# The block of r, k and w that a chunk loads: 128 rows of three padded pieces in place of 112 unbroken rows

## The chip, the cores and the metric

The kernel runs on one core of a Trainium2 chip. The metric is the device time of one execution in microseconds, so lower is better. Five engines work side by side: TensorE (PE, whose weight loads are listed apart as PEld), VectorE (DVE), ScalarE (ACT), GpSimd (POOL) and SyncE (SP, which here issues nearly all DMAs). Sixteen DMA engines move the data between DRAM and the on-chip memory SBUF, which has 128 rows (partitions).

## What is computed

Two stages follow each other. The first is a recurrence over 768 positions for 4 batches and 8 heads of width 48, with a state of 48 by 48 for each batch and head that is multiplied by w at each position. The second is a feed-forward layer on the 3072 by 384 result, with a hard-swish between its two products.

```python
for t in range(S):
    kt, vt, rt, wt = (k[:, :, t], v[:, :, t], r[:, :, t], w[:, :, t])
    cur = np.einsum('bhd,bhe->bhde', u[None] * kt, vt)
    y[:, :, t] = np.einsum('bhd,bhde->bhe', rt, state + cur)
    state = wt[:, :, :, None] * state + np.einsum('bhd,bhe->bhde', kt, vt)
...
h = x @ w_in                                 # (3072, 384) @ (384, 2048)
g = h * np.clip(h + 3.0, 0.0, 6.0) / 6.0
out = g @ w_out                              # (3072, 2048) @ (2048, 384)
```

## The kernel before

**Chunks.** The 768 positions of a batch are cut into 6 chunks of 128, so there are 24 chunks. Chunks of two batches alternate, and four chunks make one block of 512 tokens for the feed-forward layer. For a chunk, r, k and w are needed with the 48 channels of a head on partitions. Four heads lie on partitions 0 to 47 and the other four on 64 to 111, so 112 partitions (`PR`) are used, and `P` is 4. The host writes this layout into one DRAM array, `feat`: a chunk has 112 rows, and each row holds 512 values of r, 512 of k, and 520 of w (eight halves of 64 positions, each with a leading 0) and a last zero, 1545 floats or 6180 bytes without a break.

**The load of a chunk** is `load_feat`, line 343. It is one DMA on SP (line 349) of 112 rows of 6180 bytes into a buffer named `feat_in`. Chunk 0 is split: its w first (line 346, 521 floats of a row), then its r and k (line 354, 1024 floats of a row). Three buffers of the name `feat_in` take turns; later in the program the same buffers also take 128-row, 6144-byte reloads of w and of the weights for a range check (lines 919 and 924), which DVE reduces. Beside the block, a chunk loads its v (`v_in`, line 361, 128 rows) and, from chunk 9 on, r and k with positions on partitions (`rk_in`, line 366).

**What reads the block.** DVE runs two scans over w, `E` from the back (line 428) and `W` from the front (line 437). `K` is k times E (line 448) and `R` is r times W (line 452); both are on DVE for chunks 0 to 6 and on POOL from then on. For chunks 0 to 8 DVE also makes `rk`, r times k (line 461), from the block; PE reduces it with u (line 473, into `ps`). PE then makes the scores of a chunk (line 498), turns K (line 514), and makes the chunk's output (lines 576 and 585, into `y_ps` or a `bank`) and its addition to the state (line 598).

**Weights.** `w_in` and `w_out` arrive as 64-bit floats in pieces named `bits` (line 391, 768 KB each), and are rebuilt as 32-bit floats on ACT (lines 400 and 405, into `more`) and DVE (line 411 into `top`, line 415 into `w_in` or `w_out`). These DMAs stand on SP's queue between the loads of the first chunks.

**The feed-forward layer.** Block 0 multiplies by w_in and w_out directly (lines 714 and 733). Later blocks use sums of blocks of the operands and fewer products (lines 829 and 884), with the sums and the hard-swish on DVE and ACT (lines 776 to 869).

**What sets the order.** Every step is added to a plan with its engine, an assumed duration and its needs. The order of all steps is one fixed table of numbers, `ORDER`, so each engine's order of instructions doesn't depend on the plan's durations. In the first 60 us of the plan, PE gets matmuls of the identity matrix without use (line 1260, into `bankS`) wherever the plan expects it to wait; their number is set when the program is built.

**A second path.** A flag that the range check sets chooses `general_path`, a slower way for extreme values of w. With these inputs it is not run.

Of the kernel before, what the change touches and what calls it, by code (L numbers as in the profile page):

```python
# [8 lines left out]
F32 = mybir.dt.float32  # L9
# [11 lines left out]
L = 128  # L21
HL = L // 2
GP = 64
# [220 lines left out]
def fast_path(tc, feat, tok, wflat, ub, ug, moe_w_in, moe_w_out, out, flag, n_chunks):  # L244
# [3 lines left out]


    nc = tc.nc  # L250
    NT, PR, nf = feat.shape
    HD = tok.shape[3]
    D = PR - GP
    H = HD // D
    P = H // 2
# [11 lines left out]
    with ExitStack() as ctx:  # L267
        const = ctx.enter_context(tc.tile_pool(name="const", bufs=1))
        io = ctx.enter_context(tc.tile_pool(name="io", bufs=3))
# [6 lines left out]
        chunk_of = [(i // NSEQ * 2 + i % 2) * n_chunks + i % NSEQ // 2 for i in range(NT)]  # L276
# [8 lines left out]
        st = [dict() for _ in range(NT)]  # L285
# [50 lines left out]


        n = P * L
        plan.ring("feat", 3)
        plan.ring("tok", 3)  # L340
        plan.ring("rk_in", 2)

        def load_feat(i):
            a = io.tile([PR, nf], F32, name="feat_in")
            if i == 0:
                nc.sync.dma_start(out=a[:, 2 * n:], in_=feat[chunk_of[i], :, 2 * n:])
                nc.scalar.dma_start(out=u_col, in_=ug)
            else:
                nc.sync.dma_start(out=a, in_=feat[chunk_of[i]])
            st[i].update(a=a, r=a[:, :n].rearrange("q (x t) -> q x t", t=HL),  # L350
                         k=a[:, n:2 * n].rearrange("q (x t) -> q x t", t=HL), w=a[:, 2 * n:])

        def load_rest():
            nc.sync.dma_start(out=st[0]["a"][:, :2 * n], in_=feat[chunk_of[0], :, :2 * n])

        def load_u():
            nc.sync.dma_start(out=u_bc, in_=ub.to_broadcast([128, HD]))
# [612 lines left out]
        def when(i):  # L970

            bk, c = divmod(i, BC)
            return BASE[bk] - LAG - (BASE[bk] - BASE[bk - 1]) / BC * (BC - 1 - c) if bk else -99.0
# [20 lines left out]
        for i in range(NT):  # L994
            t = when(i)
            k = START[i] if i < len(START) else when(i - 2) - AHEAD
            first, last = is_first(i), is_last(i)
            dve = i < EARLY
            behind = [f"fetch{BEHIND[i]}"] if i < len(BEHIND) and BEHIND[i] >= 0 else []
            plan.add(f"feat{i}", "SP", 0.45 if i else 1.15, do(load_feat, i), behind + [f"feat{i - 1}"] * (i > 0) + ["later"] * (i == 1), k - 20, kb=735 if i else 294,  # L1000
                     hold=[("feat", [f"K{i}", f"R{i}"] + [f"own{i}"] * (i < BY_PE))])
            plan.add(f"tok{i}", "SP", 0.45, do(load_tok, i), behind + [f"feat{i}"] * (i > 1) + ["later"] * (i < 2), k - 19.9, kb=320,
# [25 lines left out]
            t = k + 1 if i < len(START) else t  # L1028
# [25 lines left out]
            bk, c = divmod(i, BC)  # L1054
# [34 lines left out]

        plan.add("u", "SP", 0.45, load_u, ["fetch3"], -60.0, kb=320)  # L1090
        plan.add("later", "SP", 0.45, load_rest, ["feat0"], key=-999.0, kb=630)

        for j in range(len(pairs)):
            t = CONV[0] + j * CONV[1]
# [12 lines left out]
        for f in range(NFC):  # L1107
            for c0, c1 in parts_of[f]:
                m, x = c1 - c0, c0 // BY_SUM
                k = UP[2 * x] + f * UP[2 * x + 1] + (c0 % BY_SUM)  # L1110
# [7 lines left out]
        for c in classic:  # L1118
            for q in range(HF):
                k = D0 + c * D0 / BC + q * 1.29  # L1120
# [36 lines left out]
        for bk in range(NB):  # L1157
# [7 lines left out]
            for d in range(2 * (bk > 0)):  # L1165
                at = K + U_ / 2 * d
                u, r = f"up{bk}.{d}.", f"read{bk}.{d}."
                name = lambda x: u + str(x) if isinstance(x, int) else r + x
# [41 lines left out]
            for p in range(2 * (bk > 0)):  # L1210
# [4 lines left out]
                d_, r, g_ = f"down{bk}.{p}.", f"out{bk}.{p}.", f"sum{bk}.{p}."  # L1215
# [26 lines left out]
        for k, (which, j) in enumerate(vets):  # L1242
            i = 8 + k // 2
# [23 lines left out]
def general_path(tc, feat, tok, ug, moe_w_in, moe_w_out, out, n_chunks):  # L1267
# [7 lines left out]


    nc = tc.nc
    NT, PR, nf = feat.shape
    HD = tok.shape[3]
    D = PR - GP  # L1280
    H = HD // D
    P = H // 2
# [1 line left out]
    DFF = moe_w_in.shape[1]  # L1284
    NCC, NFC = DM // 128, DFF // 128
    MB = GBC * L
    n2 = 2 * P * L

    with ExitStack() as ctx:
        const = ctx.enter_context(tc.tile_pool(name="g_const", bufs=1))  # L1290
        io = ctx.enter_context(tc.tile_pool(name="g_io", bufs=3))
# [4 lines left out]
        st = [dict() for _ in range(NT)]  # L1296

        def load(i):
            a = io.tile([PR, 3, P, L], F32, name="rkw_in")
            b = io.tile([L, H, D], F32, name="v_in", bufs=4)  # L1300
            nc.sync.dma_start(out=a[:, 0:2].rearrange("q c p t -> q (c p t)"), in_=feat[i, :, :n2])
            nc.sync.dma_start(out=a[:, 2].rearrange("q p (a t) -> q (p a) t", a=2),
                              in_=feat[i, :, n2:nf - 1].rearrange("q (x t) -> q x t", x=2 * P)[:, :, 1:])
            nc.sync.dma_start(out=b.rearrange("s h d -> s (h d)"), in_=tok[i, :, 2, :])
            st[i].update(R=a[:, 0], K=a[:, 1], tot=a[:, 2], v=b)

        load(0)
        ub_sb = const.tile([PR, P, 2], F32, name="ub_sb")
        nc.sync.dma_start(out=ub_sb, in_=ug)
        load(1)  # L1310

        w_in = const.tile([128, NFC, NCC, 128], F32, name="w_in_g")
# [24 lines left out]
        for i in range(NA):  # L1337
            a = const.tile([128, 2, P, L], F32, name=f"scores_{i}")
# [147 lines left out]
        for i in range(NT):  # L1486
            if i + 2 < NT:
                load(i + 2)
            own(i)
            for l in range(LEVELS):  # L1490
                score(i, l)
                merge(i, l)
            read(i)
            write(i)
            turn(i)
            if i % GBC == GBC - 1:
                for f in range(NFC):
                    up(i // GBC, f)
                for c in range(GBC):
                    down(i // GBC, c)  # L1500
# [3 lines left out]
def kernel(  # L1504
# [25 lines left out]
    flags = ctx.enter_context(tc.tile_pool(name="flags", bufs=1))  # L1530
    flag = flags.tile([1, 1], I32, name="flag")
    fast_path(tc, feat, tok, wflat, ub, ug, moe_w_in, moe_w_out, out, flag, n_chunks)
    bad = nc.values_load(flag[0:1, 0:1], min_val=0, max_val=128)
    with tc.If(bad > 0):
        general_path(tc, feat, tok, ug, moe_w_in, moe_w_out, out, n_chunks)
# [64 lines left out]
```

## Time and profile before

| | |
|---|---|
| three runs | 544.54, 546.07, 546.16 us (median 546.07) |
| profiled execution | 545.16 us, of which the span from the first to the last instruction is 543.4 us |
| PE busy | 533.5 us, 98% of the span |
| PE weight loads busy | 468.2 us, 86% |
| DVE busy | 423.5 us, 78% |
| ACT busy | 267.7 us, 49% |
| POOL busy | 111.2 us, 20% |
| DMA | 64.08 MB in 23270 packets |
| granted TensorE clock, mean | 0.999 |

The page of the profile gives the busy time of each engine, the span in 40 slices, the DMA queues, the chain of work that ended last (followed back from the last instruction through whatever released each step), the costliest groups of instructions and the DMA issues with their median time from issue to landing. The trace behind it answers further questions: who waited for whom, what happened in a stretch, how fast the DMA engines moved in it. An arrow in a name reads "output <- inputs". A wait in brackets is idle time of the engine just before an instruction, with what ended it.

### The profile page before, as it was taken

To read this page: it belongs to the slowest core of one execution; us is meant where nothing else is said; L and a number is where in the kernel's file an instruction comes from. 1 tells how busy PE (TensorE), PEld (TensorE's weight loads), DVE (VectorE), ACT (ScalarE), POOL (GpSimd) and SP (SyncE) were. 2 spreads that over 40 slices of the span, in tenths; PEclk is the share of its full clock that TensorE was granted. 3 is DMA by queue.
4 is the path that set the end of the run, shared out by engine and by line. 5 is a ranking of instruction groups with operands and counts; after the bars stand their busy time and mean duration, and the time that the engine had idled before them with its cause. 6 is when DMAs were issued, how large, how long until landed. Compare 5 with 4: busy or idle time off the path is not lost.

```text
span 543.4 us, 13407 instructions
## 1 busy us (share of the span) xinstructions
PE 533.5 (98%) x5558; PEld 468.2 (86%) x5558; DVE 423.5 (78%) x726; ACT 267.7 (49%) x657; POOL 111.2 (20%) x111
## 2 busy tenths in 40 slices
PE   8999999999999999999999999999999999999995
PEld 8898876666888999888999888999888999888995
DVE  7898999777899977999978989968889724478531
ACT  3898885333655334546525557425455324264200
POOL 2000002456221126211613154025310000000000
PEclk9999999999999999999999999999999999999999
DMA  8979853434253262655044865032510001000001
GB/s 266 301 192 301 282 178 97 117 111 119 58 144 108 70 179 95 225 190 162 23 146 154 268 212 143 0 106 84 178 58 1 2 16 30 31 0 2 1 29 36
DMA packets 23270, 64.08 MB, mean 118 GB/s; under 512 B 3216, under 2 KB 10544, under 8 KB 23200
## 3 DMA queue, kind: packets, MB, share of 16 engines
q1 hardware_dynamic: 23072, 63.12, 38.0%
q8 instruction: 46, 0.75, 0.6%
q14 instruction: 24, 0.20, 0.1%
q10 hardware_dynamic: 128, 0.00, 0.0%
HBM read 57.31 MB, written 4.72 MB: 114 GB/s over the span
## 4 chain that ended last, share of the span: by engine, by line
PE 93%; DVE 3%; ACT 1%; DMA 1%; issue 1%; POOL 0%; POOLq 0%; DVEq 0%
PE bank L884 28%; PE bank L829 25%; PE bank L714 8%; PE bank L733 8%; PE bankS L884 5%; PE bankS L829 5%; PE y_ps L576 2%; PE y_ps L598 2%; PE bank L498 2%; PE ps L514 2%; PE bankS L1260 2%; PE y_ps L585 2%; DVE g L846 1%; PE ps L473 1%; DMA feat_in<-in_moe_w_out_dram 1%; DVE g L854 1%
## 5 line engine op out<-in xcount | busy, mean ns | idle before, releaser
L850 ACT ACTIVATE clip<-g,three 128x512 f32<-128x512 f32 x80 | 57.0, 722 | 54.1 <-DVE g L846 44.7
L846 DVE TENSOR_TENSOR g<-bank,g 128x512 f32<-128x512 f32 x80 | 53.7, 685 | 10.4 <-PE bank L829 9.2
L854 DVE SCALAR_TENSOR_TENSOR g<-clip,g 128x512 f32<-128x512 f32 x80 | 54.9, 700 | 5.8 <-ACT clip L850 5.8
L884 PE MATMUL bank<-w_out,g 128*128 128x192 f32 x320 | 57.3, 327 | 0.0
L489 ACT ACTIVATE A<-eyes,dg 128x64 f32<-128x64 f32 x192 | 49.5, 338 | 10.9 <-PE y_ps L585 10.6
L884 PEld LDWEIGHTS bank<-w_out,g 128*128 128x128 f32 x320 | 52.8, 190 | 1.2 <-DVE g L854 0.3
L448 POOL TENSOR_TENSOR K<-feat_in,E 112x512 f32<-112x512 f32 x17 | 22.3, 1309 | 133.7 <-DVE W L452 84.8
L714 PE MATMUL bank<-xT,w_in 128*128 128x256 f32 (+1 forms) x216 | 45.6, 362 | 1.2 <-ACT more L405 1.2
L681 ACT COPY xT<-y_ps 48x256 f32<-48x256 f32 x88 | 32.1, 365 | 27.7 <-PE y_ps L585 26.9
L733 PE MATMUL bank<-w_out,g 128*128 128x384 f32 x128 | 43.8, 491 | 0.0
L714 PEld LDWEIGHTS bank<-xT,w_in 128*128 128x128 f32 x216 | 36.5, 190 | 5.8 <-ACT more L405 1.3
L829 PE MATMUL bank<-xT,w_in 128*128 128x256 f32 x160 | 40.4, 380 | 0.1
L844 ACT COPY g<-bank 128x512 f32<-128x512 f32 x50 | 28.8, 582 | 21.2 <-PE bank L829 17.8
L733 PEld LDWEIGHTS bank<-w_out,g 128*128 128x128 f32 x128 | 23.5, 190 | 14.2
L428 DVE TENSOR_TENSOR_SCAN E<-feat_in,back 112x520 f32<-112x520 f32 x24 | 31.4, 1310 | 4.1 <-DMA feat_in<-in_feat_dram 3.1
L900 ACT ACTIVATE o<-bank 128x192 f32<-128x192 f32 x30 | 9.9, 329 | 49.7 <-PE bank L884 49.6
L829 PEld LDWEIGHTS bank<-xT,w_in 128*128 128x128 f32 x160 | 30.1, 190 | 4.5 <-ACT g L844 0.7
L437 DVE TENSOR_TENSOR_SCAN W<-feat_in,start 112x520 f32<-112x520 f32 x24 | 31.4, 1307 | 0.8 <-PE y_ps L576 0.6
L452 POOL TENSOR_TENSOR W<-feat_in,W 112x512 f32<-112x512 f32 x17 | 22.8, 1342 | 44.3 <-DVE W L437 44.3
L829 PE MATMUL bank<-xT,bits 128*128 128x256 f32 x120 | 30.8, 380 | 0.0
L505 DVE COPY_PREDICATED A<-mask,bank 128x256 f32<-128x256 uint8 x48 | 18.6, 441 | 14.9 <-PE bank L498 14.7
L884 PE MATMUL bank<-more,g 128*128 128x192 f32 x160 | 28.7, 328 | 0.0
(290 smaller groups left out, 1135.2 us busy)
## 6 DMA issues: line engine op xcount, KB each, us to landing
feat_in<-in_feat_dram SPq DMA_DIRECT2D x23, 675.9 KB, 5.6
bits<-in_moe_w_in_dram SPq DMA_DIRECT2D x8, 768.0 KB, 10.5
bits<-in_moe_w_out_dram SPq DMA_DIRECT2D x8, 768.0 KB, 5.6
feat_in<-in_moe_w_in_dram SPq DMA_DIRECT2D x8, 768.0 KB, 4.6
feat_in<-in_moe_w_out_dram SPq DMA_DIRECT2D x8, 768.0 KB, 5.0
rk_in<-in_tok_dram SPq DMA_DIRECT2D x15, 384.0 KB, 6.0
v_in<-in_tok_dram SPq DMA_DIRECT2D x24, 192.0 KB, 4.9
out_dram<-o SPq DMA_DIRECT2D x24, 192.0 KB, 2.1
```

What stands on the lines that cost most here:

```text
L428: nc.vector.tensor_tensor_scan(out=E_[:, ::-1], data0=d["w"][:, :0:-1], data1=back.rearrange("q p t -> q (p t)")[:, ::-1], initial=0.0, op ...
L437: nc.vector.tensor_tensor_scan(out=W_, data0=d["w"][:, :-1], data1=starts[i % 2].rearrange("q p t -> q (p t)"), initial=0.0, op0=ALU.mult, ...
L489: nc.scalar.activation(out=d["A"][:, h, :], in_=eyes, func=ACT.Copy, scale=d["dg"][:, h])
L681: nc.scalar.copy(out=blocks[bk]["xT"][g * GP:g * GP + D, :, at:at + HL], in_=st[i]["y_ps"][a][(g ^ a) * GP:(g ^ a) * GP + D, :, :])
L714: nc.tensor.matmul(h_ps[:, :(c1 - c0) * L], lhsT=w_in[:, f // 2, j, f % 2, :], rhs=b["xT"][:, j, c0 * L:c1 * L], start=(j == 0), stop=(j = ...
L733: nc.tensor.matmul(b["o", c][:, :DM], lhsT=g_of(0, f, c), rhs=w_out[:, f, :], start=(f == 0), stop=(f == NFC - 1))
L829: nc.tensor.matmul(b["p", d, c][:, z * HB:(z + 1) * HB], lhsT=weight(W_PLACE[r], d)[:, z, :], rhs=x_at(bk, X_PLACE[r]), start=fresh and z ...
L844: nc.scalar.copy(out=out_, in_=src)
L846: nc.vector.tensor_tensor(out=out_, in0=src, in1=out_of(bk, d, other), op=ALU.add if sign > 0 else ALU.subtract)
L850: nc.scalar.activation(out=c, in_=out_of(bk, d, u), func=ACT.Relu, bias=three, scale=twice)
L854: nc.vector.scalar_tensor_tensor(out=g, in0=blocks[bk]["r", d, u], scalar=6.0, in1=g, op0=ALU.min, op1=ALU.mult)
L884: nc.tensor.matmul(b["d", p, to][:, :h], lhsT=a, rhs=w(), start=(f == 0 and k in (1, 5)), stop=(f == HF - 1 and k in (2, 3, 4)), skip_grou ...
```

## The change

In DRAM a chunk's block becomes 128 rows of three pieces: r, k and w. A piece has room for 528 floats (2112 bytes), and rows 112 to 127 hold zeros. The load of a chunk moves 521 floats (2084 bytes) of each piece, to the same places in a buffer of 128 rows and three pieces of 528 floats. The split load of chunk 0 has 128 rows as well: 521 floats of w, and then 512 of r and of k. The views that the engines read are the first 112 rows, with r, k and w at a distance of 2112 bytes from each other instead of 2048. A `feat_in` buffer takes 6336 bytes of a partition instead of 6180. A chunk's load thus has 384 pieces in place of 112 and moves 800,256 bytes in place of 692,160. The other path reads the same array. The table `ORDER`, the plan's numbers and each engine's order of instructions, with what each waits for, are the same in both programs.

```diff
         def load_feat(i):
-            a = io.tile([PR, nf], F32, name="feat_in")
+            b = io.tile([feat.shape[1], 3, feat.shape[3]], F32, name="feat_in")
+            a = b[:PR]
             if i == 0:
-                nc.sync.dma_start(out=a[:, 2 * n:], in_=feat[chunk_of[i], :, 2 * n:])
+                nc.sync.dma_start(out=b[:, 2, :nw], in_=feat[chunk_of[i], :, 2, :nw])
                 nc.scalar.dma_start(out=u_col, in_=ug)
             else:
-                nc.sync.dma_start(out=a, in_=feat[chunk_of[i]])
-            st[i].update(a=a, r=a[:, :n].rearrange("q (x t) -> q x t", t=HL),
-                         k=a[:, n:2 * n].rearrange("q (x t) -> q x t", t=HL), w=a[:, 2 * n:])
+                nc.sync.dma_start(out=b[:, :, :nw], in_=feat[chunk_of[i], :, :, :nw])
+            st[i].update(b=b, r=a[:, 0, :n].rearrange("q (x t) -> q x t", t=HL),
+                         k=a[:, 1, :n].rearrange("q (x t) -> q x t", t=HL), w=a[:, 2, :nw])
 
         def load_rest():
-            nc.sync.dma_start(out=st[0]["a"][:, :2 * n], in_=feat[chunk_of[0], :, :2 * n])
+            nc.sync.dma_start(out=st[0]["b"][:, :2, :n], in_=feat[chunk_of[0], :, :2, :n])
...
-    end = _np.zeros((NT, GP + D, 1), w.dtype)
+    n, nw = P * L, 2 * P * (HL + 1)
+    feat = _np.zeros((NT, 128, 3, -(-(nw + 1) // 16) * 16), w.dtype)
...
-    laid["feat"] = _np.concatenate([rk.reshape(NT, GP + D, -1), ws.reshape(NT, GP + D, -1), end], axis=2)
+    feat[:, :GP + D, :2, :n] = rk.reshape(NT, GP + D, 2, n)
+    feat[:, :GP + D, 2, :nw] = ws.reshape(NT, GP + D, nw)
+    laid["feat"] = feat
```

In the fast path `nw` is 2·P·(HL+1)+1, or 521, and `n` is 512.

More of the change, by code (lines that the diff above doesn't have):

```diff
@@ L250, in fast_path @@
     nc = tc.nc
-    NT, PR, nf = feat.shape
+    NT, PR = feat.shape[0], ug.shape[0]
     HD = tok.shape[3]
@@ L338, in fast_path @@
         n = P * L
+        nw = 2 * P * (HL + 1) + 1
         plan.ring("feat", 3)
@@ L1277, in general_path @@
     nc = tc.nc
-    NT, PR, nf = feat.shape
+    NT, PR = feat.shape[0], ug.shape[0]
     HD = tok.shape[3]
@@ L1286, in general_path @@
     MB = GBC * L
-    n2 = 2 * P * L
+    n = P * L
     with ExitStack() as ctx:
@@ L1300, in load @@
             b = io.tile([L, H, D], F32, name="v_in", bufs=4)
-            nc.sync.dma_start(out=a[:, 0:2].rearrange("q c p t -> q (c p t)"), in_=feat[i, :, :n2])
+            nc.sync.dma_start(out=a[:, 0:2].rearrange("q c p t -> q c (p t)"), in_=feat[i, :PR, :2, :n])
             nc.sync.dma_start(out=a[:, 2].rearrange("q p (a t) -> q (p a) t", a=2),
-                              in_=feat[i, :, n2:nf - 1].rearrange("q (x t) -> q x t", x=2 * P)[:, :, 1:])
+                              in_=feat[i, :PR, 2, :2 * P * (HL + 1)].rearrange("q (x t) -> q x t", x=2 * P)[:, :, 1:])
             nc.sync.dma_start(out=b.rearrange("s h d -> s (h d)"), in_=tok[i, :, 2, :])
```

## The prediction

> **What bounds the kernel now.** I read the page's busy times and slices first, then who PE waited for, then what waits for the block's loads, and last the two stretches at the front where such a load is near PE's work.
>
> ```profile
> span 543.4 us, 13407 instructions
> PE 533.5 (98%) x5558; PEld 468.2 (86%) x5558; DVE 423.5 (78%) x726; ACT 267.7 (49%) x657; POOL 111.2 (20%) x111
> PEclk9999999999999999999999999999999999999999
> DMA  8979853434253262655044865032510001000001
> ```
>
> PE is busy 98% of the span at full clock in all 40 slices. The DMA engines are busy 7 to 9 tenths of the first five slices (68 us) and mostly less than half of the later ones. A busy PE could still hide short waits, so the second view is the list of PE's waits.
>
> ```profile
> engine line waited for: us in total, times, longest us
> PE bankS L1260 <- POOL ident masks.py:199: 1.4, 1, 1.4
> PE bank L714 <- ACT more L405: 1.2, 1, 1.2
> PE bank L829 <- DVE g L846: 0.5, 1, 0.5
> PE bank L829 <- DVE T__3533 L776: 0.2, 1, 0.2
> PE bank L884 <- DVE S__4096 L869: 0.2, 1, 0.2
> ```
>
> These are all: 3.5 us, and none ends with a DMA. The first, 1.4 us, is the start of the program. What is left to win from any transfer, however fast, is 1.2 + 0.5 + 0.2 + 0.2 = 2.1 us. Loads of the block are waited for elsewhere, on DVE:
>
> ```profile
> DVE E L428 <- DMA feat_in<-in_feat_dram: 3.1, 3, 1.2
> ...
> DVE o L902 <- DMA feat_in<-in_feat_dram: 2.0, 1, 2.0
> ...
> DVE rk L461 <- DMA feat_in<-in_feat_dram: 0.7, 1, 0.7
> ```
>
> That is 5.8 us on an engine that is idle for over a fifth of the span. PE is the bound from 1.4 us to the end, and the change touches nothing that PE executes.
>
> **The change part by part.** *The load itself.* The page's DMA issues, with KB and the median time to landing:
>
> ```profile
> feat_in<-in_feat_dram SPq DMA_DIRECT2D x23, 675.9 KB, 5.6
> ...
> feat_in<-in_wflat_dram SPq DMA_DIRECT2D x6, 768.0 KB, 4.4
> ...
> feat_in<-in_feat_dram SPq DMA_DIRECT2D x1, 448.0 KB, 3.9
> feat_in<-in_feat_dram SPq DMA_DIRECT2D x1, 227.9 KB, 3.0
> ```
>
> The block's load of 112 rows takes 5.6 us, and a larger one of 128 rows into the same buffers 4.4 us. How fast the engines move the pieces shows in two stretches at the front in which the DMA share is full; for each, the row of the windows and then the packets:
>
> ```profile
> 12.00:14.00 2.00, 2.00 (x25) 1.76 (x25) 2.00 (x5) 1.49 (x7) 0.00 (x0) 1.00 1.04 386
> DMA packets 393, 0.77 MB, mean 386 GB/s; under 512 B 16, under 2 KB 17, under 8 KB 393
> ```
>
> ```profile
> 15.50:16.50 1.00, 0.91 (x49) 0.77 (x47) 0.28 (x2) 1.00 (x2) 0.00 (x0) 1.00 1.05 237
> DMA packets 48, 0.24 MB, mean 237 GB/s; under 512 B 3, under 2 KB 3, under 8 KB 48
> ```
>
> From 12 to 14 us the packets average 2 KB (0.77 MB in 393), as the weights' pieces do that stand between the blocks on the queue, and the rate is 386 GB/s. From 15.5 to 16.5 us the packets average 5 KB, those of a chunk's block among them, and the rate is 237 GB/s with the engines just as busy. So the large packets of the 112 rows are the slow ones here. The new block's 800,256 bytes at 386 GB/s take 2.07 us, where 692,160 bytes at 237 take 2.92: 0.85 us less for a load. The other bound gives the new block the old rate: 800,256 / 237 = 3.38 us, 0.46 us more. I take the first, because its packets (2 KB, 128 rows) are nearest to the new ones (2084 bytes, 128 rows).
>
> By the Trainium skill, page "DMA: Bandwidth & Descriptors", section "How a descriptor splits into AXI transactions", a piece costs 32-byte beats, and one that doesn't start on a multiple of 256 bytes also pays for the bytes before its start. As an estimate from that page, an engine would handle 24 pieces of about 69 beats (1656) in place of 7 rows of about 198 (1386), so the new load would take 19% longer, some 0.55 us. The trace speaks against beats as what sets this load: the 768 KB reload needs more of them by the same count (8 rows of 192, 1536) and lands 1.2 us sooner.
>
> *Chunk 0, split.* Its w grows from 112 to 128 rows, 33,344 bytes, which is 0.09 us at 386 GB/s and 0.14 at 237, ahead of the first scan. Rows of the timeline at the front:
>
> ```profile
> 6.54 0.67 DVE L461 TENSOR_TENSOR rk<-feat_in 112x512 f32<-112x512 f32 x1
> ...
> 8.03 0.63 PE L473 MATMUL ps<-u_col,rk 112*64 112x2 f32 x16
> ...
> 9.64 1.24 DVE L428 TENSOR_TENSOR_SCAN E<-feat_in,back 112x520 f32<-112x520 f32 x1 [1.22 <-DMA feat_in<-in_feat_dram]
> ...
> 11.03 0.65 DVE L461 TENSOR_TENSOR rk<-feat_in 112x512 f32<-112x512 f32 x1
> ...
> 12.13 0.63 PE L473 MATMUL ps<-u_col,rk 112*64 112x2 f32 x16
> ```
>
> For chunk 0, rk is done at 7.21 us and PE reads it at 8.03, after its matmuls without use: 0.8 us of cover. Cost nothing.
>
> *Chunk 1.* DVE waited 1.22 us for this load before 9.64 us; most of that goes. PE reads this rk at 12.13, and it was done at 11.68. An earlier load lengthens this cover of 0.45 us; PE meanwhile works through its fixed list, so it gains nothing.
>
> *The weights behind the blocks.* Pieces of w_in queue behind the blocks, so they land sooner too. PE's one long wait after the start stands where they are used:
>
> ```profile
> 20.34 0.64 ACT L664 COPY xT<-y_ps 64x192 f32<-64x192 f32 x2
> ...
> 21.00 1.07 ACT L400 ACTIVATE more<-bits 128x768 uint16<-128x768 uint32 x1
> ...
> 21.95 1.04 ACT L405 ACTIVATE more<-bits 128x768 bf16<-128x768 int32 x1
> 22.20 0.69 DVE L461 TENSOR_TENSOR rk<-feat_in 112x512 f32<-112x512 f32 x1 [0.68 <-DMA feat_in<-in_feat_dram]
> ...
> 23.21 1.60 PE L714 MATMUL bank<-xT,w_in 128*128 128x128 f32 x12 [1.18 <-ACT more L405]
> ...
> 24.75 0.40 PE L473 MATMUL ps<-u_col,rk 112*64 112x2 f32 x8
> ```
>
> The 1.18 us before 23.21 end with ACT's L405, by this profile. ACT goes from the copy L664 straight to L400 and L405, with no wait of its own, so earlier weights don't start them earlier. The block of chunk 2 held DVE for 0.68 us, and its rk is done at 22.89, 1.86 us before PE reads it at 24.75. Bounds for the front: a gain of 0 and of 1.2 us. I take 0, the row of ACT being nearest.
>
> *Later loads.* From 60 us on the DMA engines are mostly idle, and PE's three waits there (0.9 us) end with DVE's sums and gates. The 2.0 us that DVE's L902 waited ended with no wait on PE. I take 0, with 0 and 0.9 us as bounds.
>
> *Readers and buffers.* The block's tile and its readers, with the shortest, median and longest time:
>
> ```profile
> L452 DVE TENSOR_TENSOR W<-feat_in,W x7: 684/686/692, 7.1 to 88.1; 112x512 f32<-112x512 f32 x7
> L448 DVE TENSOR_TENSOR K<-feat_in,E x7: 668/686/687, 7.7 to 64.1; 112x512 f32<-112x512 f32 x7
> ```
>
> L452 reads r at the row's start and L448 reads k at 2048 bytes, in the same 686 ns: the place in the row made no difference. Cost 0; bounded by the 16 ns between their shortest times, at most 24 x 5 such readings, 1.9 us in all on DVE and POOL, in either direction, and not on PE's path.
>
> *SP.* The issue of a load of the block, then of one with three pieces per row, both as shortest, median and longest time in ns, and last SP's longest wait in total:
>
> ```profile
> L349 SPq DMA_DIRECT2D feat_in<-in_feat_dram x23: 327/330/1158, 1.7 to 354.2; - x23
> ```
>
> ```profile
> L391 SPq DMA_DIRECT2D bits<-in_moe_w_in_dram x8: 368/378/1228, 2.7 to 39.1; - x8
> ```
>
> ```profile
> SPq L744 <- DVE o L902: 98.1, 9, 45.0
> ```
>
> Issuing three pieces for each row takes 378 ns in place of 330, 0.05 us for each of 23 loads. Behind them on SP stand the loads of v and r, k; SP waits 98 us for results to store, so 1.1 us on it cost nothing.
>
> **The sum** against the profiled execution: 545.16 + 0 (chunk 0) + 0 (front) + 0 (later) = 545.16, with 2.1 us as the most that can go. That execution lies 0.9 us below the median of the runs, 546.07; the middle of all four is 545.6, and this is the forecast.
>
> **The rivals.** *The front gives its wait back (faster).* If the wait before 23.21 us in truth depended on transfers (the weights, or PE's own instructions, which come through the same full DMA engines), and DVE's earlier work also ended the three later ones, all 2.1 us go: 543.5. For it: an instruction transfer stands in just that stretch, from 20.4 to 22 us.
>
> ```profile
> q8 instruction: 1, 0.02, 4.9%
> ```
>
>  Against it: PE's waits end with ACT and DVE by the profile, and ACT had no wait. Half of it, 1.2 us, would still be within 0.3%, which is 1.64 us and about what a measurement of this kernel can tell from no change. Chance 0.10.
>
> *More pieces are slower pieces (slower).* In the first five slices the block's loads share full queues with the weights. If the new load keeps 237 GB/s, each takes 0.46 us more. It decides from the point where chunk 1's load is over 0.45 us later than now: then PE waits at 12.13 us for rk. Six loads up to chunk 6 would add 2.8 us to the queue, 0.45 of it covered: 2.3 us, 547.9. The Trainium skill's count of beats, above, would act in this way. Against it: 2 KB packets at 386 GB/s in the same queue, and the 1.86 us of cover at chunk 2. Chance 0.08.
>
> *The loads don't land sooner at all.* Something other than packets and rows, such as the weights beside them, may set the 5.6 us. Then DVE's waits stay and the time is 545.6 as well. For it: the reloads with 4.4 us mostly run alone. Against it: the two stretches above, equally full. Chance 0.14.
>
> **The numbers.** Forecast as argued, loads sooner and hidden: 0.68, at 545.6. With the third rival, no change has 0.82, faster 0.10, slower 0.08. The range goes from 543.5, where all waits that could go are gone, to 547.1, the highest run (546.16) and the 0.9 us between the profiled execution and the median on top; it leaves out the slower rival.
>
> **What would show it.** After: the block's load lands in well under 5.6 us though it is larger; the DVE waits of 3.1, 2.0 and 0.7 us shrink; PE's waits still sum to about 3.5 us with the same releasers, and PE is busy for the same 533.5 us. The forecast is wrong if the span differs by over 1.6 us: then the list of PE's waits must have lost or gained a row of that size, or PE's busy time must have changed, which no row here foresees.

## The result, and the profile after

After the change the time is 544.72 us (median of 20 runs, 543.66 to 545.79); before it is 547.25 us (median of 20, 544.54 to 556.36). The ratio is 0.9948, with an interval from 0.993 to 0.9967. The comparison leaves out runs over 1.5% above the quickest of the same kernel, so the ratio doesn't count before's highest times. The change makes the kernel 0.3 to 0.7% faster. The forecast time, 545.6, is 0.9 us off and its range holds the result, but the forecast of no change is wrong.

What the medians don't tell is the spread: after's 20 runs lie within 2.1 us, and before's spread over 11.8. The execution of before that was profiled took 545.16 us, among its quickest, and the one of after 545.69. So the two profiles alone can't show the gain. First the page after, in the lines that answer to those of before, with the issues of the block's loads and of w_in's pieces:

```profile
span 544.0 us, 13407 instructions
...
PE 532.9 (98%) x5558; PEld 466.7 (86%) x5558; DVE 425.1 (78%) x726; ACT 268.1 (49%) x657; POOL 112.9 (21%) x111
...
DMA  8949753333252253645044854032510001000001
...
feat_in<-in_feat_dram SPq DMA_DIRECT2D x23, 781.5 KB, 5.0
bits<-in_moe_w_in_dram SPq DMA_DIRECT2D x8, 768.0 KB, 6.7
```

PE's busy time is that of before within 0.6 us. The load of a block takes 5.0 us though it is larger (5.6 before), and the pieces of w_in, which stand behind the first blocks, land in 6.7 us (10.5 before). The same stretch of the front as in the prediction, at full DMA share:

```profile
15.50:16.50 1.00, 1.00 (x75) 0.90 (x66) 0.00 (x0) 1.00 (x3) 0.00 (x0) 1.00 1.06 395
```

It runs at 395 GB/s, where it was 237. Then DVE's waits for a block, and all of PE's waits:

```profile
DVE o L904 <- DMA feat_in<-in_feat_dram: 2.0, 1, 2.0
DVE E L430 <- DMA feat_in<-in_feat_dram: 1.1, 1, 1.1
```

```profile
PE bankS L1262 <- POOL ident masks.py:199: 1.4, 1, 1.4
PE bank L831 <- DVE g L848: 0.8, 2, 0.5
PE bank L716 <- issue: 0.7, 1, 0.7
PE ps L475 <- DVE rk L463: 0.4, 1, 0.4
PE y_ps L600 <- ACT kvs L611: 0.4, 1, 0.4
PE bank L831 <- DVE T__3533 L778: 0.2, 1, 0.2
PE bank L886 <- DVE S__4096 L871: 0.2, 1, 0.2
```

DVE's 3.1 us shrank to 1.1, and rk's 0.7 is gone. PE's waits sum to 4.1 us, no less than before's 3.5. One line differs in kind: the wait ahead of the first up-product (L716, which is L714 of before) is now 0.7 us and ends with "issue", that is with nothing the profile shows, where before's ended "with ACT more L405".

### The profile page after: what moved, and what is told of

It reads as the page before. It is cut to its first block, busy times and chain, and to the rows that moved or that the text cites. A ratio compares the mean times of both kernels' runs of the same rounds, so it can differ in the third digit from the quotient of the medians.

```text
span 544.0 us, 13407 instructions
## 1 busy us (share of the span) xinstructions
PE 532.9 (98%) x5558; PEld 466.7 (86%) x5558; DVE 425.1 (78%) x726; ACT 268.1 (49%) x657; POOL 112.9 (21%) x111
## 4 chain that ended last, share of the span: by engine, by line
PE 87%; DVE 7%; DMA 2%; issue 1%; ACT 1%; DVEq 0%; ACTq 0%
PE bank L886 28%; PE bank L831 22%; PE bank L735 7%; PE bank L716 7%; PE bankS L886 5%; PE bankS L831 4%; DVE g L848 3%; PE y_ps L578 2%; PE y_ps L600 2%; PE bank L500 2%; PE ps L516 2%; PE y_ps L587 2%; DVE g L856 1%; DMA bits<-in_moe_w_out_dram 1%; PE bankS L1262 1%
## 5 line engine op out<-in xcount | busy, mean ns | idle before, releaser
L856 DVE SCALAR_TENSOR_TENSOR g<-clip,g 128x512 f32<-128x512 f32 x80 | 56.2, 716 | 5.8 <-ACT clip L852 5.8
L886 PE MATMUL bank<-w_out,g 128*128 128x192 f32 x320 | 57.3, 327 | 0.0
L886 PEld LDWEIGHTS bank<-w_out,g 128*128 128x128 f32 x320 | 52.8, 190 | 1.2 <-DVE g L856 0.3
L450 POOL TENSOR_TENSOR K<-feat_in,E 112x512 f32<-112x512 f32 x17 | 23.1, 1361 | 133.8 <-PE bank L500 128.0
L716 PE MATMUL bank<-xT,w_in 128*128 128x256 f32 (+1 forms) x216 | 45.5, 362 | 0.7 <-issue 0.7
L716 PEld LDWEIGHTS bank<-xT,w_in 128*128 128x128 f32 x216 | 36.5, 190 | 5.3 <-issue 0.9
L831 PE MATMUL bank<-xT,w_in 128*128 128x256 f32 x160 | 40.5, 381 | 0.4 <-DVE g L848 0.4
L831 PEld LDWEIGHTS bank<-xT,w_in 128*128 128x128 f32 x160 | 30.0, 190 | 5.2 <-DVE g L848 0.8
L454 POOL TENSOR_TENSOR W<-feat_in,W 112x512 f32<-112x512 f32 x17 | 22.8, 1342 | 44.3 <-DVE W L439 44.3
L831 PE MATMUL bank<-xT,bits 128*128 128x256 f32 x120 | 30.9, 381 | 0.0
L886 PE MATMUL bank<-more,g 128*128 128x192 f32 x160 | 28.7, 328 | 0.0
```

The lines of the kernel that those rows point to most:

```text
L716: nc.tensor.matmul(h_ps[:, :(c1 - c0) * L], lhsT=w_in[:, f // 2, j, f % 2, :], rhs=b["xT"][:, j, c0 * L:c1 * L], start=(j == 0), stop=(j = ...
L831: nc.tensor.matmul(b["p", d, c][:, z * HB:(z + 1) * HB], lhsT=weight(W_PLACE[r], d)[:, z, :], rhs=x_at(bk, X_PLACE[r]), start=fresh and z ...
L856: nc.vector.scalar_tensor_tensor(out=g, in0=blocks[bk]["r", d, u], scalar=6.0, in1=g, op0=ALU.min, op1=ALU.mult)
L886: nc.tensor.matmul(b["d", p, to][:, :h], lhsT=a, rhs=w(), start=(f == 0 and k in (1, 5)), stop=(f == HF - 1 and k in (2, 3, 4)), skip_grou ...
```

## The experiments

The theory after this look (theory A in the expectations): before's spread comes from late loads at the front, and it is the 112 rows that make them late. The rivals: the length and alignment of the pieces does it and not the rows (B); or the runs differ for a reason of the chip or its clock that isn't the change (C). The first four kernels of the table test this. Their profiles gave the fuller theory that the others test (theory F): PE's wait ahead of the first up-product is a wait for PE's own instructions. They come through the same DMA engines (the queue named "instruction"), behind the loads of the blocks; blocks of 112 rows move slowly and make them late, by an amount that differs between executions, and a long standstill costs more than its length. Its rivals are that PE waits there for weights (W), that later loads do it (L), or that the sum of all early lateness does (S).

| kernel | rows, chunks 0 to 4 | rows, later | time, us | ratio to before on the same chip |
|---|---|---|---|---|
| before_again | 112 | 112 | 547.01 | 0.999 [0.9954, 1.0026] |
| after_again | 128 | 128 | 544.74 | 0.9924 [0.9895, 0.9952] |
| rows_only | 128, unbroken | 128, unbroken | 544.51 | 0.9908 [0.9872, 0.9944] |
| pieces_only | 112, pieces | 112, pieces | 549.84 | 1.0006 [0.9976, 1.0037] |
| front_112 | 112, pieces | 128, pieces | 549.42 | 1.003 [0.9984, 1.0076] |
| mid_112 | 112 in chunks 2 and 3 only | 128 | 551.88 | 1.0051 [1.0003, 1.0099] |
| late_112 | 128 | 112, pieces | 543.91 | 0.9929 [0.9893, 0.9965] |
| late_112_again | 128 | 112, pieces | 544.01 | 0.9875 [0.9814, 0.9936] |
| late_whole | 128, unbroken | 112, unbroken | 543.38 | 0.9868 [0.9807, 0.9929] |
| after_third | 128 | 128 | 544.63 | 0.9883 [0.9822, 0.9944] |
| fewer_fillers | 112 | 112 | 546.75 | 0.9985 [0.9943, 1.0026] |
| pause | 128 | 128 | 551.07 | 1.0067 [1.0041, 1.0094] |

The first four ran on one chip, front_112, mid_112, late_112 and fewer_fillers on a second, the others on a third. Each ran 12 times, but rows_only 9 times and late_112_again, late_whole and after_third 6 times. Every kernel whose first five blocks have 128 rows is faster than before, except pause, in which PE is held up; none of the others is.

**Rows or pieces: rows_only and pieces_only.** The change has two parts, and each was done alone. rows_only keeps the unbroken row of 6180 bytes and adds the 16 rows of zeros:

```diff
-            a = io.tile([PR, nf], F32, name="feat_in")
+            b = io.tile([feat.shape[1], nf], F32, name="feat_in")
+            a = b[:PR]
...
-                nc.sync.dma_start(out=a, in_=feat[chunk_of[i]])
+                nc.sync.dma_start(out=b, in_=feat[chunk_of[i]])
```

> The rows alone: 128 rows, each 6180 bytes unbroken, the last 16 zeros. Theory A (the spread of before's runs comes from late loads at the front, and it is the 112 rows that make the loads slow): the loads of chunks 1 and 2 land by about 8.5 and 19 us as with the whole change (9.5 and 22.2 before), the runs stay under 546 us, ratio to before about 0.995. Rival B (the length of the pieces is what makes them slow): landings stay at about 9.5 and 22 us, runs spread from 544.5 to over 550, ratio 1.000. Rival C (the spread is of the chip or its clock and no kernel differs): ratio within 0.3% of 1, whatever the landings do.

pieces_only is the changed kernel with 112 rows of three pieces:

```diff
-    feat = _np.zeros((NT, 128, 3, -(-(nw + 1) // 16) * 16), w.dtype)
+    feat = _np.zeros((NT, GP + D, 3, -(-(nw + 1) // 16) * 16), w.dtype)
```

> The pieces alone: 112 rows of three pieces of 2084 bytes, 2112 bytes apart. Theory A (112 rows are what is slow): landings and spread as before, ratio 1.000. Rival B (long pieces are what is slow): chunks 1 and 2 land by about 8.3 and 18.5 us, since 14% fewer bytes move than with 128 rows, the runs stay under 546 us, ratio about 0.995. Rival C (chip or clock): ratio within 0.3% of 1.

The stretch from 15.5 to 16.5 us and the median load, in rows_only:

```profile
15.50:16.50 1.00, 0.99 (x68) 1.00 (x72) 0.00 (x0) 1.00 (x2) 0.00 (x0) 1.00 1.07 413
```

```profile
feat_in<-in_feat_dram SPq DMA_DIRECT2D x23, 772.5 KB, 4.8
```

And in pieces_only:

```profile
15.50:16.50 1.00, 1.00 (x55) 0.87 (x58) 0.22 (x1) 1.00 (x2) 0.00 (x0) 1.00 1.07 254
```

```profile
feat_in<-in_feat_dram SPq DMA_DIRECT2D x23, 683.8 KB, 6.1
```

With 128 rows, whole or in pieces, the stretch moves at 413 and 395 GB/s; with 112 rows, whole or in pieces, at 237 and 254. The stretches don't hold the same loads (133 of rows_only's 173 packets there are under 2 KB, as those of v are), so the block's own loads are the better measure. From issue to landing, the loads of chunks 1 and 2 take 7.8 and 15.9 us in before, 7.3 and 14.8 in pieces_only, 6.7 and 12.4 in after, and 6.1 and 12.2 in rows_only. The pieces do little here, and the rows do nearly all of it, in the load and in the time: rows_only gives 0.9908, a larger gain than the expected 0.995, and pieces_only 1.0006. In rows_only PE doesn't wait for its first up-product at all, and in pieces_only it waits longest of all; the rows of the timeline, start and duration first, rows_only's ahead of pieces_only's:

```profile
21.43 1.60 PE L715 MATMUL bank<-xT,w_in 128*128 128x128 f32 x12
```

```profile
24.62 2.24 PE L716 MATMUL bank<-xT,w_in 128*128 128x128 f32 x12 [2.93 <-issue]
```

**The two kernels again: after_again and before_again.** Both without an edit, for a second and third profile of what the first pair showed as nearly equal.

> The whole change once more, on the chip of the other runs of this call. Theories A and B: ratio 0.993 to 0.997 and no run over 546.5 us. Rival C (the difference lay in which chip or clock the runs met): ratio within 0.3% of 1 and the same spread as the kernel before.

> The kernel before, timed against itself: ratio 1.000 by any theory; its runs show the spread on this chip. Theories A and B expect a third or more of the runs over 547 us. If the profiled execution is one of the slow ones, A and B expect its extra time as waits of PE in the first 60 us with loads of the block or the weights behind them, and rival C expects the same waits of PE as before (3.5 us) with a lower granted clock.

after_again has no wait ahead of L716. Six of before_again's 12 runs took over 547 us, none of after_again's. before_again took 547.16 us in its profiled execution, 2 us more than the one that the prediction was made against, and shows what that one lacked. Its up-product:

```profile
24.21 2.93 PE L714 MATMUL bank<-xT,w_in 128*128 128x128 f32 x12 [2.25 <-issue]
```

The wait is 2.25 us (1.18 in the first profile), it ends with "issue", and the same 12 products then take 2.93 us in place of 1.60. The granted clock, last but two in a row of the windows, says why; before_again, then the first profile of before:

```profile
24.00:27.40 3.40, 3.19 (x20) 2.96 (x22) 1.10 (x1) 0.59 (x2) 0.00 (x0) 0.51 1.04 373
```

```profile
24.00:27.40 3.40, 3.40 (x43) 3.26 (x41) 3.37 (x8) 2.82 (x13) 0.00 (x0) 1.00 1.06 382
```

After the longer standstill TensorE gets half its clock for 3.4 us and does 20 matmuls where it did 43 (not all of one size). So this wait cost 2.25 us and then half of 3.3 us (3.4 x 0.49 / 0.5): 3.9 us in all. The same in pieces_only, for a longer stretch:

```profile
25.00:36.00 11.00, 11.00 (x73) 10.54 (x73) 4.01 (x8) 5.14 (x21) 0.00 (x0) 0.53 0.79 236
```

Eleven microseconds at a mean of 0.53 are 10.3 us at half clock (11 x 0.47 / 0.5), so 5.2 us lost, behind a wait of 2.93.

**What PE waited for.** The last wait of this kind in before ends, by the prediction's profile, with ACT's L405. Two views speak against that. First, the instruction transfer that is in flight just ahead. In a window of 0.1 us that holds only its start, its row gives its whole time as a share of 16 engines: share x 1.6 us is its duration, and its start is known to 0.1 us (0.15 for late_112). Rows for before from 20.5, for before_again from 21.5, for pieces_only from 21.9, and for rows_only from 17.8 us:

```profile
q8 instruction: 1, 0.02, 78.8%
```

```profile
q8 instruction: 1, 0.02, 79.6%
```

```profile
q8 instruction: 1, 0.02, 83.8%
```

```profile
q8 instruction: 1, 0.02, 81.3%
```

| kernel | transfer starts, us | lasts | ends about | PE goes on at | later by |
|---|---|---|---|---|---|
| before | 20.5 | 1.26 | 21.8 | 23.21 | 1.4 |
| before_again | 21.5 | 1.27 | 22.8 | 24.21 | 1.4 |
| pieces_only | 21.9 | 1.34 | 23.3 | 24.62 | 1.3 |
| mid_112 | 21.2 | 1.28 | 22.5 | 24.07 | 1.6 |
| front_112 | 21.5 | 1.10 | 22.6 | 24.05 | 1.4 |
| fewer_fillers (below) | 21.8 | 1.25 | 23.1 | 24.50 | 1.4 |
| after | 19.7 | 1.11 | 20.9 | 22.16 | 1.3 |
| after_again | 19.1 | 1.10 | 20.2 | no wait | |
| late_112_again | 19.4 | 1.09 | 20.5 | no wait | |
| pause | 18.8 | 1.09 | 19.9 | no wait here | |
| late_112 | 18.5 | 1.09 | 19.6 | no wait | |
| after_third | 18.5 | 1.09 | 19.6 | no wait | |
| late_whole | 18.0 | 1.06 | 19.1 | no wait | |
| rows_only | 17.8 | 1.30 | 19.2 | no wait | |

In all seven profiles with the wait, PE goes on 1.3 to 1.6 us after the transfer's end, and where that end came by about 20.5 us there is no wait. What differs is when the transfer starts, not how long it takes: the 46 instruction transfers of a page take 1.1 us on average (0.6% of 16 engines' 544 us). Second, the count of work that PE did up to the end of its wait, from the start of the program; before, then before_again:

```profile
0.00:23.20 23.20, 20.43 (x346) 18.67 (x346) 17.21 (x33) 14.74 (x37) 3.01 (x15) 1.00 0.94 268
```

```profile
0.00:24.20 24.20, 20.35 (x346) 18.59 (x346) 19.14 (x36) 14.77 (x37) 3.01 (x15) 0.99 0.95 255
```

PE stops after the same 346 matmuls and 346 weight loads each time. That is so in after, pieces_only, mid_112 and front_112 too, whose programs have the same order. The same count, taken up to the starts of the transfers, tells what holds this one up. Leaving fewer_fillers aside, whose instructions are others, the transfer two further on (32.7 to 41.0 us) starts after 461 to 465 matmuls in all 13 profiles, and the one behind that after 631 to 636: they go by where PE is. The one in question starts after 283 to 298 matmuls with 128 rows, and after 298 to 346 with 112 rows in the loads of chunks 2 and 3. So with 112 rows it starts up to 63 matmuls later in PE's work than in rows_only.

**Is it the place in the stream or the step? fewer_fillers.** If PE stands still at a place in its stream of instructions and not at a step of the work, then the wait must move to a later step when instructions ahead of it go. This kernel is before without nine of the matmuls that have no use:

```diff
+            if 22 <= n_ <= 30:
+                return
```

> The kernel before with its 112-row loads as they are, but nine of PE's matmuls without use left out between 11 and 18 us (36 instructions in all), so that the end of the instructions that PE holds falls after the first up-product instead of ahead of it. Theory F: the wait of 1.2 to 2.9 us before the first up-product goes or falls under 1 us, the clock isn't halved, and the runs gather at 544 to 546.5 us, ratio 0.990 to 0.996, though the loads land as late as before (chunk 2 at 21 to 22 us). Rival W (PE waits there for weights or for ACT's work on them): the wait and the spread stay, ratio 0.998 to 1.002, or over 1 because PE is idle where it had work without use.

The timeline from the first up-product on:

```profile
21.64 1.58 PE L714 MATMUL bank<-xT,w_in 128*128 128x128 f32 x12 [0.64 <-DVE w_in L415]
23.27 0.39 PE L473 MATMUL ps<-u_col,rk 112*64 112x2 f32 x6
24.50 0.51 PE L473 MATMUL ps<-u_col,rk 112*64 112x2 f32 x10 [0.84 <-issue]
```

The up-product now starts at 21.64 us, and the wait for "issue" stands 18 matmuls later, in the middle of L473's sixteen. Nine fillers are 18 matmuls on this page (5540 in place of 5558). And the count to the end of the wait:

```profile
0.00:24.45 24.45, 20.45 (x346) 17.91 (x346) 18.08 (x34) 16.07 (x44) 3.01 (x15) 1.00 0.95 274
```

Again 346 and 346. So it is a place in the stream: the wait is for instructions. That they come on this queue shows in the page, where fewer_fillers, with 36 instructions fewer, all of them PE's, has 45 instruction transfers in place of 46. In the same profile the up-product waits 0.64 us for w_in, which shows how little else held it. As a cure, the edit failed: the expected gain isn't there (0.9985, with 1 inside the interval), and 3 of its 12 runs have a mean clock of 0.989 or less. PE now reached the place at 23.66 us, 1.6 later than in before, and its instructions came later still in this execution, which was one of the quicker ones (545.49 us; the 12 go from 544.64 to 553.65). Why the time didn't follow is not settled by one profile.

**Does the standstill itself cost the time? pause.** The changed kernel, with a standstill put in: six copies on ACT of the input of the first up-products onto itself, for which PE's second six products wait. No work is left out.

```diff
+            if f == 0 and c0 == 0:
+                x = b["xT"][:, :NCC, :L]
+                for _ in range(6):
+                    nc.scalar.copy(out=x, in_=x)
```

> The change as it is, with six copies on ACT of the first up-product's input onto itself put ahead of that product, some 0.5 us each, so that PE stands still there for about 3 us (0 to 0.9 us with the change) although no load is slow. Theory F (standing still for over 2 us halves the clock): in most executions a half-clock stretch of 3.4 us or more follows, mean clocks of 0.985 to 0.995, median 547.5 to 552, that is 3 to 7 us over the whole change, of which some 2.5 are the wait itself. Rival D (the halved clock has to do with the DMA load or with the slow loads, not with PE's standing still): only the wait is added, 546.5 to 547.5, and the clock stays at 0.997 or over.

It takes 551.07 us (549.42 to 552.78), 6.4 more than after_third on the same chip; all 12 runs have a mean clock of 0.989 to 0.996, where after_third's six have 0.996 to 1.000. The timeline, and the clock behind it:

```profile
23.02 3.22 ACT L718 COPY xT<-xT 128x384 f32<-128x384 f32 x6 [0.88 <-PE bank L720]
...
26.30 1.65 PE L720 MATMUL bank<-xT,w_in 128*128 128x128 f32 x6 [3.37 <-ACT xT L718]
```

```profile
25.00:36.00 11.00, 9.70 (x80) 9.33 (x81) 6.73 (x13) 7.81 (x28) 0.00 (x0) 0.69 0.49 165
```

A wait of 3.37 us, then 6.8 us at half clock (11 x 0.31 / 0.5), 3.4 lost: 6.8 us together, near the 6.4 measured. So a standstill costs about twice its length here even when no load is slow. By the same count before_again's cost 1.7 times its length (3.9 us for 2.25) and pieces_only's 2.8 times (8.1 for 2.93).

**Which blocks: front_112, mid_112, late_112.** The changed kernel with 112 rows in some loads only. The condition is `i < 5` in front_112 (and chunk 0's two loads as well), `i in (2, 3)` in mid_112, `i >= 5` in late_112:

```diff
-                nc.sync.dma_start(out=b[:, :, :nw], in_=feat[chunk_of[i], :, :, :nw])
+                q = PR if i in (2, 3) else 128
+                nc.sync.dma_start(out=b[:q, :, :nw], in_=feat[chunk_of[i], :q, :, :nw])
```

> The change, but with the loads of chunks 0 to 4 cut to 112 rows, later ones of 128. Theory F: as with 112 rows throughout, median 547 to 551, ratio 0.998 to 1.003, mean clocks of 0.986 to 0.997, a wait of over 2 us before the first up-product in most executions. Rival L (later loads matter): ratio 0.993 to 0.997.

> The change, but with the loads of chunks 2 and 3 alone cut to 112 rows; they are on the way at 14 to 25 us, when the instructions for the first up-product are asked for. Theory F: most of the loss comes back from two of 24 loads: median 547 or more, runs to 551, mean clocks under 0.996 in a third of the runs or more, a wait of 1 to 3 us before the first up-product. Rival S (the sum of all early lateness counts, the weights' landing above all): two of six early loads bring back a third at most, ratio to before under 0.996.

> The change, but with the loads of chunks 5 and later cut to 112 rows (three pieces, the last 16 rows of the buffer not written). Theory F (at the front, PE's next 16 KB of instructions come late through DMA engines that the 112-row loads keep full; PE stands still before its first up-product, and where that lasts over about 2 us the clock is halved for a while): the front is as with the whole change, so the median is 544 to 545.5, no run over 547, ratio 0.990 to 0.996. Rival L (the later loads matter too, by waits of DVE and POOL): half or more of the gain is lost, ratio over 0.996.

In mid_112 the wait is back with 112 rows in two loads of 24, and the halved clock behind it:

```profile
PE bank L717 <- issue: 2.1, 1, 2.1
```

```profile
24.00:27.40 3.40, 3.33 (x24) 3.11 (x24) 1.09 (x1) 0.74 (x4) 0.00 (x0) 0.52 1.05 383
```

front_112 has the same wait of 2.0 us. In late_112, with 112 rows in the 19 later loads, all of PE's waits after the start are these:

```profile
PE bank L832 <- DVE T__3533 L779: 0.2, 1, 0.2
PE bank L887 <- DVE S__4096 L872: 0.2, 1, 0.2
```

So the effect comes from the first five loads, and 112 rows in two of them are enough to lose the gain. mid_112 and front_112 came out no better than before; their ratios (1.0051 and 1.003) don't differ from each other.

**A version from this: late_112_again and late_whole.** If the first loads do it all, the 16 rows and the pieces are not needed later. late_whole is before with 128 unbroken rows for the first five chunks only (`b` is the buffer of 128 rows, `a` its first 112):

```diff
-                nc.sync.dma_start(out=a, in_=feat[chunk_of[i]])
+                q = 128 if i < 5 else PR
+                nc.sync.dma_start(out=b[:q], in_=feat[chunk_of[i], :q])
```

> Loads of 128 rows for chunks 0 to 4, and 112 rows (three pieces) from chunk 5 on, once more, on one chip with the whole change. In the two profiled executions of the whole change, 0.5 to 1 us of what the front gains is given back where PE waits for DVE at 194 and 253 us, and in the one with late loads of 112 rows it isn't. If that is so by rule, the median lies 0.5 to 1 us under that of the whole change (543.7 to 544.2); if it was chance, the two are within 0.3 us.

> Unbroken rows of 6180 bytes, 128 of them for chunks 0 to 4 and 112 from chunk 5 on: the kernel before with nothing changed but 16 more rows in the first five loads. Theory F: the whole gain, median 543.5 to 544.8, ratio 0.988 to 0.996, no run over 546.5.

> The whole change, as the measure for the other three on this chip: median 544.3 to 545.2 by any theory.

late_whole has the lowest time of all, 543.38 us (542.71 to 544.40), 1.25 under after_third (543.73 to 545.23) and 0.6 under late_112_again (543.08 to 544.93). It is a little under the expected 543.5 to 544.8 and beats before by 0.7 to 1.9%. Against the changed kernel the six runs of each overlap a little, so this is likely a gain and not a certain one.

## Where the prediction held and where it failed, point by point

**The number.** The time is near the forecast and inside the range, but that is partly luck. No change was forecast from 545.6 us, the middle of four executions of before that were among its quicker ones. By 20 runs before is at 547.25 us; no change from there would lie 2.5 us over what was measured and outside the range. The prediction's own sign of being wrong, a difference of over 1.6 us, is met by the medians and not by the two profiled spans (543.4 and 544.0 us).

**The bound.** Right: PE is busy for 532.9 us (533.5 before), and no block's load is waited for on PE. But "what is left to win from any transfer, however fast" was put at 2.1 us, the sum of waits in one execution. This step failed. before_again's profile alone has 3.9 us in one wait and the clock behind it. The sum was made against 545.16 us, an execution in which the wait happened to be 1.18 us and the clock wasn't halved. The three runs shown, up to 546.16, gave no hint of what 20 showed.

**The load.** Right in size: 395 GB/s measured where 386 was taken, and DVE's waits shrank from 3.1 to 1.1 us and from 0.7 to 0, but the one of 2.0 us, which was to shrink too, stayed. Wrong in one reason: the 5 KB packets were called the slow ones. rows_only has the same unbroken rows and moves at 413 GB/s, and pieces_only has 2 KB pieces and moves at 254. The count of beats from the Trainium skill, page "DMA: Bandwidth & Descriptors", section "How a descriptor splits into AXI transactions", doesn't set this load either: by the estimate from it the new load would take 19% longer, and those of chunks 1 and 2 take 14 and 22% less (6.7 and 12.4 us in after, 7.8 and 15.9 in before).

**Chunk 0, chunk 1.** PE waits 0.4 us for chunk 0's rk, which the prediction had covered by 0.8. That isn't the load, since rk starts at 6.54 us in both kernels. PE was earlier, as its first 34 matmuls without use took 5.45 us and not 6.67:

```profile
1.43 5.45 PE L1262 MATMUL bankS<-ident 128*128 128x128 f32 x34 [1.43 <-POOL ident masks.py:199]
```

Over the executions of all kernels this takes from 5.4 to 6.9 us, before_again 6.62 and after_again 6.50 among them, so it doesn't belong to the change. It also accounts for part of what the two first profiles differ by at the up-product: PE starts it 1.05 us sooner in after (22.16 against 23.21), of which 0.43 come from the shorter wait and 0.62 from PE's being there earlier.

**The front: the step that failed.** "The 1.18 us before 23.21 us end with ACT's L405, by this profile", and since ACT had no wait of its own, the gain was taken as 0, between 0 and 1.2 us. The releaser was a coincidence: L405 ended at 22.99 us, and the wait is for instructions, as fewer_fillers shows. Its end does depend on transfers. The prediction had this as its first rival, "PE's own instructions, which come through the same full DMA engines", had quoted the row of that transfer, and gave it 0.10. It also priced that rival by the wait's length in one execution, 1.2 us, and called this within 0.3%. Measured, the wait is 1.2 to 2.9 us with 112 rows (0.84 in fewer_fillers) and 0 to 0.75 with 128, and those of 1.98 us and more were followed by a halved clock.

**Where the 0.5% comes from.** The clocks of before's runs are at hand for the chip of the first experiments, where after_again is 0.8% (4 us) faster. Of the 27 quicker of before's 32 runs there, 13 have a mean clock of 0.994 or less and the median is 0.995; after_again's 12 all have 0.997 or more. One thousandth of mean clock is 0.5 us here, so the clock accounts for 1 to 2 us of the difference. The shorter wait, 1.2 to 2.3 us in the two profiles of before against 0 to 0.75 in three of after, is about the size of the rest. That division is an estimate; no run has the one without the other on before's loads.

**Later loads, readers, SP.** The later loads and the readers came out as said, to the size of a microsecond: the median reading of r and of k takes 686 and 687 ns. SP's issue was priced too low: a load of the new block takes 606 ns to issue (median, line 351), where 378 were taken and 330 measured before. That is 0.28 us for each of 23 loads in place of 0.05, 6.3 us in all, and still no wait of PE ends with it. Something is given back by the later loads: the first profile of after has 0.4 us at L600 and 0.8 at L831 where before has 0 and 0.5 (after_again and after_third have 0.3 at L831 and 0.2 to 0.3 at L886). The profiles of late_112 and late_112_again have none of these, and late_112_again is 0.6 us under after_third. That 128-row loads later on cost this is only read from profiles, and it is near what six runs can tell.

**More pieces are slower.** This rival fell: the load with more pieces landed sooner. **The loads don't land sooner at all** fell too.

**Left open.** Why 112 rows move at about 60% of the rate of 128 in full queues. How far the standstill has to go for the clock to be halved, and what sets for how long: 0.75 and 1.18 us had no such effect, 1.98 us and more had it. That the instruction transfer starts late because it stands behind the blocks on a DMA engine is argued, not shown: the counts of matmuls at its start say that it is held up when chunks 2 and 3 have 112 rows, but no view gives the moment when it was asked for or the engine that it stood on.

## What to carry to other kernels

A wait in a profile of one execution is a sample. Where full DMA queues stand beside a busy TensorE, look for the transfer on the instruction queue and for the granted clock behind each wait of PE, and take a second profile, best of a slower execution, before pricing the wait at its length. A releaser named for a wait is worth a check: count the engine's instructions up to its end in two executions, or remove a few ahead of it, and see whether the wait stays with the step or with the count. And a load of 112 rows may be made 128 at the price of 14% more bytes where the queues are full: here that raised the rate of a full stretch from 237 to 395 GB/s.

## What the runs showed of the hardware

**PE can stand still for its own instructions.** They arrive in packets of 16 KB (0.75 MB in 46 in the page of after) on a queue of their own through the same DMA engines:

```profile
q8 instruction: 46, 0.75, 0.6%
```

A packet beside full queues took 1.1 to 1.3 us, as much as over the whole span, and PE went on 1.3 to 1.6 us after its end. The Trainium skill, page "Runtime: NRT & Kernel Launch", section "Instruction fetch mechanics", has the refill in blocks of 16 KiB, as measured, and its cost as mostly hidden: in rows_only it is hidden, in pieces_only it is 2.93 us and another 5.2 of halved clock.

**The clock is halved in steps.** The stretches at half clock were 3.3 us (before_again), 6.8 (pause) and 10.3 (pieces_only), close to one, two and three times 3.4. In every profile the recorded changes of the clock lie whole multiples of 3.41 us apart: in before_again down at 23.90 and up at 27.31 us, in pieces_only down at 25.40 and up at 35.64. So where a standstill falls between two such points may count as well as its length; that is not tested here. The Trainium skill, page "TensorE: Matmul & The Clock Gate", section "What's actually happening", has a window of 3.4 us that runs freely and the halved clock after an idle window; the lengths agree with that, but standstills of 2.0 to 2.3 us were enough here, well short of a whole window.

**Rows decide the rate of a load in full queues.** In the stretch from 15.5 to 16.5 us, kernels with 112 rows in the block that is on its way move 232 to 286 GB/s (six profiles) and those with 128 rows 388 to 413 (eight), with the engines as busy (shares of 1.03 to 1.11); rows_only has the same bytes in a row as before.
